# Attention plus a channel MLP on one core: the last 64 keys of a head scored into both partition halves, and q and k loaded whole

## The chip, the cores and the metric

One core of a Trainium2 chip runs the whole program. The metric is the device time of one execution in microseconds (us); the number before is the median of three runs. Engines are named as in the profile: PE is the matrix engine (PEld its weight loads), DVE the vector engine, ACT the scalar engine, POOL GpSimd, SP the engine that issues the DMAs. A "product" is one matmul instruction or, where two matmuls on two halves of the array run side by side, that pair.

## The reference, cut to what matters

```python
def _attn_ref(q, k, v):                    # q, k, v: (8, 12, 448, 64) float32
    scores = 1/np.sqrt(64) * np.matmul(q, k.transpose(0, 1, 3, 2)) - np.log(448)
    attn = 1.0 / (1.0 + np.exp(-scores))   # a sigmoid, no sum over the keys
    return np.matmul(attn, v)
def _moe_ref(x, U, V, w_ch1, w_ch2):       # x: (8, 448, 768), the 12 heads side by side
    h = x.transpose(0, 2, 1) @ U @ V       # rank 32 over the sequence
    u = x + h.transpose(0, 2, 1)
    return u + np.maximum(u @ w_ch1, 0.0) @ w_ch2     # 768 -> 3072 -> 768
```

Eight batches; in each 12 heads, taken as 6 pairs; 448 keys and 448 queries of 64 numbers.

## The kernel before

**Precision.** PE multiplies 16-bit numbers in one pass. A 32-bit factor is therefore split into a high and a low 16-bit part, and a product is made of three: high by high, high by low, low by high. Batches 0 to 2 skip the split in their attention and multiply 32-bit numbers directly ("whole"); batches 3 to 7, 30 pairs, use the split.

**Attention of one pair of heads** (`pair`). The two heads lie in the two halves of the 128 partitions, 64 numbers of a head in each. `loads` fetches k and q by five transfers: k and q of each head (64 rows each) and v. For a split pair ACT measures sums of magnitudes (`bound`), two small transfers through DRAM bring a scale to all partitions (`scale_by_dma`), POOL makes the high parts and DVE the low parts, into a staging tile `stg`. The 448 keys are cut into three blocks of 128 (j = 0, 1, 2) and a block of 64 (j = 3). `scores_of` makes the scores of a block, keys on the partitions, queries along the row, for both heads: for j < 3 into two banks of the accumulator memory (a buffer of `TWO`, one bank per head), for j = 3 into one bank, with head 0 in the partitions 0 to 63 and head 1 in 64 to 127. It is called for the blocks (3, 0) and then for (1, 2). ACT turns the scores into sigmoids (L642), ACT makes their high part (L662) and DVE the low part (L663, recorded under the helper's line 408). `values_of` (L552) then multiplies with v: three products of 128 x 128 for j = 3 (v holds the two heads' 64 keys as a block diagonal), and three products for each j < 3, each of two 128 x 64 matmuls, one per head: 12 products.

**Rank-32 mixing** (`mix`, `mix_half`) follows when six (or three) pairs are done. In `mix_half` a transposing DMA (L798) takes part.

**The MLP.** Batches 0 to 3 go through groups of 18 and 12 matmuls of 128 x 128 by 448 (`ffn_in`, `ffn_out`); the weights arrive as 64-bit words, are decoded (`decode`) and kept in DRAM in split form. Batches 4 to 7 go through a fast multiplication scheme of 7 instead of 8 block products at the end (`in_quad`, `out_quad`), whose inputs are formed early for batches 4 and 5 (`far_forms`, `near_forms`) and whose weight sums are made on POOL (`quarter_sums`). The MLP matmuls of one batch are what PE runs between the attention steps of later batches.

**What sets the order.** `Plan` collects every operation with its engine, a guessed cost, what it reads and writes and a priority `pos`; `Plan.order` walks through time with these costs and writes one fixed order of instructions for each engine. Every engine then runs its own list strictly in order and waits where data is missing. The constants at the top (START, DECODE, PREP, AHEAD and so on) place the priorities. The costs steer the order only; they are no part of the program that runs. Buffers (`QK`, `V32`, `STG`, `A2`, `A1`, `AT2`, `AT1`, the banks `BANK` and `TWO`) are given out by the same walk. Of the banks, 0 to 2 serve the MLP and 3 to 7 attention and mixing from batch 2 on; `TWO[2:]` are banks 4-5 and 6-7.

Transfers are all issued by SP, in its order. The line of a transfer in the profile is often that of the helper `load` (L379), that of a matmul always L395, that of a DVE remainder or POOL scaling L408 or L405: tile names tell them apart.

Of the kernel before, what the change touches and what calls it, by code (L numbers as in the profile page):

```python
# [52 lines left out]
WHOLE = 3  # L53
D2, TWO_AT = 28.077, 81.576
PLAIN = 4
LATER = [4, 3, 5, 6, 7]
TOGETHER = (2, 3, 4, 5)
BEND = 0.096
DIRECT = ()
FORMS = {1: (0,), 2: (1,), 3: (2,)}  # L60
MM = 0.190
TINY = 235

ROOM0, ROOM, AHEAD, BEFORE, D1, SOONER = 65.569, 34.316, 67.823, 41.157, 3.106, 71.183
PREP, BOUNDS, VALUES, SECOND, MIXED = 23.415, 9.75, 1.292, 4.05, 6.82
LOW_POOL = ()
MIXED1, MIX_1 = 9.523, 3.666
MIX_2, EV_IN, EV_OUT, A_OFF = 7.323, 25.524, 4.098, -0.681
START, DECODE = 53.869, 35.813
U_AT, U_STEP = 3.333, 5.172  # L70
LEAD, SUMS, STEP_K, STEP_I, FFN_LEAD = 8.152, 14.538, 16.739, 13.37, 4.0
# [22 lines left out]
class Plan:  # L94
# [13 lines left out]
    def op(self, eng, cost, fn, reads=(), writes=(), pos=0.0, slack=0.0, land=0.12, after=(), port=False):  # L108
# [19 lines left out]
        self.ops.append((eng, cost, fn, sorted(deps), pos, slack, land, tiles, port))  # L128
        return i

    def order(self):
# [10 lines left out]
        ready, end = [0.0] * n, [0.0] * n  # L142
# [6 lines left out]
        done, port, landed = [], 0.0, [0.0] * 8  # L149
# [21 lines left out]
        while len(done) < n:  # L171
            best = None
            for e, c in cand.items():
                now = []
                for i in c:
                    r = room(i)
                    if r is not None:
                        o = self.ops[i]
                        now.append((max(free[e], ready[i], r[0] + o[5] if r[1] else 0.0, port if o[8] else 0.0, landed[-8] if e == "SP" else 0.0), o[4], i))
# [17 lines left out]
            end[i] = t + o[1]  # L197
            free[e] = end[i]
            if o[8]:
                port = end[i]  # L200
            if e == "SP":
                landed.append(end[i] + o[6])
            done.append(i)
            for x in o[7]:
                x.left -= 1
                x.got.free = max(x.got.free, end[i] + o[6])
                if not x.left:
                    x.got.live = False
            for u in users[i]:
                x = self.ops[u]  # L210
                at = end[i] + (o[6] + x[5] if x[0] != e or e == "SP" else 0.0 if e == "PE" else 0.06)
# [34 lines left out]
def fused_kernel(ctx: ExitStack, tc: tile.TileContext, q, k, v, wu, wv, w1, w2, out):  # L246
# [40 lines left out]
    a_, at_ = buf("a", [12 * S], F32), buf("at", [5 * S], F32)  # L287
    A2, A1 = [Buffer(a_[:, 2 * i * S : 2 * (i + 1) * S]) for i in range(5)], [Buffer(a_[:, i * S : (i + 1) * S]) for i in (10, 11)]
    AT2, AT1 = [Buffer(at_[:, 2 * i * S : 2 * (i + 1) * S]) for i in range(2)], [Buffer(at_[:, 4 * S :])]
    QK = ring("qk", 3, [2, S], F32)  # L290
# [30 lines left out]
    for x, owners in ((STG[0].ap, STG[:1]), (STG[1].ap, STG[1:]), (at_.bitcast(F16), AT2 + AT1), (US[1].ap.rearrange("p a b c -> p (a b c)"), US[1:])):  # L321
# [30 lines left out]
    for x in QK + A2 + A1 + V32 + STG + AT2 + AT1:  # L352
# [25 lines left out]
    def load(dst, src, n, reads, writes, pos, land=2.0):  # L378
        op("SP", max(0.6, n / 0.30e6), lambda: nc.sync.dma_start(out=dst(), in_=src()), reads, writes, pos, land=land)  # L379
# [20 lines left out]
    def pe(cost, fn, reads, writes, pos, slack=0.8, after=()):  # L400
        return op("PE", cost, fn, reads, writes, pos, slack, 0.3, after)
# [31 lines left out]
    def scale_by_dma(parts, kp, n, name, pos):  # L433
# [3 lines left out]
        load(lambda: far.x, lambda: parts.x[:, :n], 0.18e6, kp, [far], pos, 4.5)  # L437
        load(lambda: row.x[:, : n * P], lambda: far.x.rearrange("p n -> (p n)").partition_broadcast(P), 0.2e6, [far], [row], pos, 5.0)
        m, x = (lambda: e.x[:, :n]), (lambda: e.x[:, n : 2 * n])
        dve(0.15 + n * 0.13, lambda: nc.vector.tensor_reduce(  # L440
# [67 lines left out]
    def shifted(at):  # L508
        pool(0.5, lambda: nc.gpsimd.memset(ux, 0.0), (), ["ux", "vraw"], at)
        dve(0.25, lambda: nc.vector.tensor_copy(ux[0:64, 0], ua[0:64, 3]), [("ua", i) for i in range(4)] + ["ux"], ["ux"], at)  # L510
        load(lambda: ux[64:128, :, 3], lambda: ua[0:64, :, 0], 0.18e6, [("ua", 0), "ux"], ["ux"], at, 4.5)
        load(lambda: ux[0:64, 1:4, 3], lambda: ua[64:128, 0:3, 0], 0.18e6, [("ua", 0), "ux"], ["ux"], at, 4.5)
# [10 lines left out]
    def loads(b, p, early):  # L523
        qk, v32 = plan.tile("qk", QK), plan.tile("v", V32)
        for h in range(2):
            for i, src in ((1, k), (0, q)):
                load(lambda i=i, h=h: qk.x[rows_of(h), i, :], lambda src=src, h=h: src[b, p, rows_of(h), h, :],
                     D * S * 4, [], [(qk, i, h)], early)
        load(lambda: v32.x, lambda: v[b, p], P * 512 * 4, [], [v32], early + 0.1)
        return qk, v32, [(qk, i, h) for i in range(2) for h in range(2)]  # L530

    def scores_of(b, js, products, kp, pos, early):

        sc = {}
        for j in js:
            if j < 3:
# [3 lines left out]
        n = 1 if b < WHOLE else 3  # L540
# [8 lines left out]
        scored.append(pe(len(js) * (4 if b < WHOLE else 3) * MM + 0.2, fn, kp, list(sc.values()), pos, after=values_ops[-2:-1] + scored[-1:]))  # L549
        return sc  # L550

    def values_of(b, products, tiles, kp, pos):  # L552
        av = plan.tile("av", PS_[b], False)

        def fn():
            n = len(products())
            for i, (x, y) in enumerate(products()):
                matmul(av.x[:, :S], x[:, 3, :], y(tiles[3], 0), start=i == 0, stop=False, skip_group_check=True)
            for j in range(3):
                for i, (x, y) in enumerate(products()):  # L560
# [787 lines left out]
```

## Time and profile before

| what | value |
|---|---|
| time, three runs | 1582.74, 1580.14, 1585.16 us; median 1582.74 |
| the profiled execution: its time / its span | 1585.82 / 1584.0 us |
| mean granted PE clock | 0.997 |
| PE busy | 1566.2 us, 99% of the span |
| DVE, ACT, POOL busy | 1093.3, 755.3, 341.2 us |
| DMA engines' busy share | 61.7% |

The page gives busy time per engine; another view gives the same for stretches of the span; the timeline gives start times of instructions, merged where neighbours are alike. Matmuls overlap in their records (each is shown with some 350 ns), so that the pace of PE is read from start to next start and not from the duration.

The stages of the span are roughly: until 105 us the start (attention of batches 0 and 1, first weights decoded), 105 to 360 us the MLP with batches 1 and 2 in between, 360 to 1000 us the MLP of batches 0 to 3 with the split attention of batches 3 to 7 in between, then to the end the MLP of batches 4 to 7.

### The profile page before, as it was taken

To read this page: it belongs to the slowest core of one execution; us is meant where nothing else is said; L and a number is where in the kernel's file an instruction comes from. 1 tells how busy PE (TensorE), PEld (TensorE's weight loads), DVE (VectorE), ACT (ScalarE), POOL (GpSimd) and SP (SyncE) were. 2 spreads that over 40 slices of the span, in tenths; PEclk is the share of its full clock that TensorE was granted. 3 is DMA by queue.
4 is the path that set the end of the run, shared out by engine and by line. 5 is a ranking of instruction groups with operands and counts; after the bars stand their busy time and mean duration, and the time that the engine had idled before them with its cause. 6 is when DMAs were issued, how large, how long until landed. Compare 5 with 4: busy or idle time off the path is not lost.

```text
span 1584.0 us, 23059 instructions
## 1 busy us (share of the span) xinstructions
PE 1566.2 (99%) x8621; PEld 760.2 (48%) x8621; DVE 1093.3 (69%) x1831; ACT 755.3 (48%) x1269; POOL 341.2 (22%) x429
## 2 busy tenths in 40 slices
PE   8999999999999999999999999899999999999999
PEld 3334544444444444444444444455555555555554
DVE  3787986747667666766568688577677677565656
ACT  6475454534574656655747667242323514121210
POOL 0100000003454351121433211045662500000000
PEclk9999999999999999999999999999999999999999
DMA  8598786525768686855566685877684563323321
GB/s 241 164 313 282 208 265 214 215 63 168 213 189 219 198 248 174 196 190 167 175 196 198 194 213 174 249 257 235 201 259 145 212 235 124 128 105 131 113 105 70
DMA packets 204112, 302.80 MB, mean 191 GB/s; under 512 B 124896, under 2 KB 171104, under 8 KB 192736
## 3 DMA queue, kind: packets, MB, share of 16 engines
q1 hardware_dynamic: 204000, 301.34, 61.7%
q8 instruction: 67, 1.10, 0.3%
q14 instruction: 45, 0.37, 0.1%
HBM read 231.11 MB, written 76.04 MB: 194 GB/s over the span
## 4 chain that ended last, share of the span: by engine, by line
PE 91%; DMA 4%; DVE 3%; ACT 1%; SPq 1%; issue 1%; POOL 0%; DVEq 0%; ACTq 0%
PE banks L395 90%; DMA w<-w_in 1%; DMA v__104<-v_in 1%; PE banks L398 1%; DVE stg__109 L408 0%; DMA w<-parked 0%; DVE a L408 0%; DMA qk__102<-ufar 0%; DMA at<-ufar 0%; DVE tiny L465 0%; ACT at L642 0%; DVE at L408 0%; DMA qk__103<-q_in 0%; DMA a<-ufar 0%; SPq L798 0%
## 5 line engine op out<-in xcount | busy, mean ns | idle before, releaser
L395 PEld LDWEIGHTS <-w__91 128*128 128x128 f16 x1683 | 163.4, 98 | 163.0 <-issue 12.1
L395 PEld LDWEIGHTS <-w__93 128*128 128x128 f16 x1620 | 156.3, 98 | 154.0 <-issue 12.1
L395 PEld LDWEIGHTS <-w__92 128*128 128x128 f16 x1620 | 157.1, 98 | 151.8 <-issue 7.3
L395 PEld LDWEIGHTS <-w__94 128*128 128x128 f16 x1557 | 150.1, 98 | 149.5 <-issue 14.0
L395 PE MATMUL banks<-h__96,w__94 128*128 128x448 f16 x753 | 152.5, 353 | 1.2 <-ACT h__95 L896 1.2
L395 PE MATMUL banks<-h__95,w__93 128*128 128x448 f16 x762 | 153.7, 353 | 0.0
L408 DVE SCALAR_TENSOR_TENSOR a<-at,a 128x448 f16<-128x448 f32 (+1 forms) x120 | 120.0, 1024 | 21.9 <-ACT a L662 21.8
L642 ACT ACTIVATE at<-banks,tiny 128x448 f32<-128x448 f32 (+1 forms) x120 | 115.6, 1002 | 33.7 <-PE banks L395 23.0
L971 POOL TENSOR_TENSOR w<-w 128x384 f32<-128x384 f32 x96 | 105.3, 1097 | 5.5
L395 PE MATMUL banks<-us__89,w__91 128*128 128x448 f16 x492 | 99.5, 353 | 0.0
L395 PE MATMUL banks<-us__90,w__91 128*128 128x448 f16 x492 | 99.4, 353 | 0.0
L395 PE MATMUL banks<-us__89,w__92 128*128 128x448 f16 x489 | 99.2, 353 | 0.0
L395 PE MATMUL banks<-us__90,w__92 128*128 128x448 f16 x489 | 99.0, 353 | 0.0
L662 ACT ACTIVATE a<-at 128x448 f16<-128x448 f32 (+1 forms) x120 | 97.6, 854 | 0.3
L405 POOL TENSOR_SCALAR tiny<-tiny 128x1 f32<-128x1 f32 (+1 forms) x90 | 25.7, 295 | 315.6 <-DVE tiny L405 286.8
L642 ACT ACTIVATE a<-banks,tiny 128x448 f32<-128x448 f32 (+1 forms) x72 | 62.8, 910 | 21.1 <-PE banks L395 18.2
L967 POOL TENSOR_TENSOR w<-w 128x384 f32<-128x384 f16 x48 | 46.5, 995 | 100.7 <-DVE xnt L975 63.2
L895 ACT ACTIVATE r__97<-banks 128x448 f32<-128x448 f32 x48 | 25.9, 540 | 71.2 <-PE banks L395 69.6
L895 ACT ACTIVATE r__98<-banks 128x448 f32<-128x448 f32 x48 | 25.9, 540 | 69.5 <-PE banks L395 69.3
L395 PEld LDWEIGHTS <-stg__108 64*128 64x128 f16 (+3 forms) x675 | 32.6, 102 | 43.1 <-issue 23.1
L395 PEld LDWEIGHTS <-stg__109 64*128 64x128 f16 (+3 forms) x675 | 32.3, 102 | 43.4 <-issue 23.9
L974 ACT CAST xnt<-w 128x1536 f16<-128x1536 f32 x24 | 35.2, 1467 | 32.5 <-POOL w L971 31.9
(927 smaller groups left out, 2811.8 us busy)
## 6 DMA issues: line engine op xcount, KB each, us to landing
w<-w_in SPq DMA_DIRECT2D x48, 768.0 KB, 5.2
forms<-xnt SPq DMA_DIRECT2D x24, 768.0 KB, 4.6
w__91<-forms SPq DMA_DIRECT2D x13, 1344.0 KB, 5.7
w__92<-forms SPq DMA_DIRECT2D x12, 1344.0 KB, 5.7
w__93<-forms SPq DMA_DIRECT2D x12, 1344.0 KB, 5.8
w__94<-forms SPq DMA_DIRECT2D x11, 1344.0 KB, 5.7
forms<-scratch SPq DMA_DIRECT2D x144, 96.0 KB, 3.7
w__91<-scratch SPq DMA_DIRECT2D x7, 1536.0 KB, 7.2
```

What stands on the lines that cost most here:

```text
L395: plan.made.append(nc.tensor.matmul(*x, **y))
L398: plan.made.append(nc.tensor.transpose(**x))
L405: return eng.tensor_scalar(out=out, in0=in_, scalar1=s1, scalar2=s2, op0=op0, **kw)
L408: return nc.vector.scalar_tensor_tensor(out=out, in0=in0, scalar=s, in1=in1, op0=op0, op1=op1)
L642: act(cost, lambda: nc.scalar.activation(out_(), in_(), AF.Sigmoid, bias=bias_s, scale=c if whole else c.x), kin + ["bias"] + kc, kout, pos)
L662: act(0.57 if j == 3 else 0.95, lambda a=a, to=to: nc.scalar.activation(half(a, 0), to.x, AF.Copy, scale=A_UP), kto, [(a, 0)], here + A_OFF)
L895: act(0.54, lambda: nc.scalar.activation(r.x, ph.x[:, :S], AF.Relu, scale=DOWN_H), [ph], [r], pos - EV_IN)
L967: pool(1.0, lambda j=j: nc.gpsimd.tensor_tensor(out=t.x[:, j], in0=quarter(j, 0), in1=quarter(j, 1), op=ALU.add), [(w, j, 0), (w, j, 1)] i ...
L971: pool(1.0, lambda o_=o_, x=x, y=y, sub=sub: nc.gpsimd.tensor_tensor(out=t.x[:, o_], in0=t.x[:, x], in1=t.x[:, y], op=ALU.subtract if sub ...
L974: act(1.45, lambda: nc.scalar.copy(o.x[:, :, :, 0], t.x.rearrange(order)), [(t, j) for j in range(4)], [(o, 0)], pos)
```

## The change

1. For the 30 split pairs ("stacked" in the code) the block j = 3 is treated as a block of 128 keys: the last 64 keys stand twice, in the rows 0 to 63 and 64 to 127. The scores of j = 3 therefore go to a two-bank buffer, one bank per head, with the same scores in both partition halves. The sigmoid and the high part are made over 896 columns of 128 partitions instead of 448. The low part then replaces the high part in the partitions 64 to 127 only, so that one 16-bit tile holds the high part above the low part. v's block for j = 3 holds the same 64 keys in both halves, both heads side by side. A product with it sums high and low part at once, so that v's high part and v's low part suffice: 2 products of two 128 x 64 matmuls each. `values_of` has 2 + 9 = 11 products.
2. k gets 64 more columns in its tile for the copy of the last keys; POOL and DVE scale 512 columns of k instead of 448.
3. q and k come in one transfer each of 128 rows instead of two of 64 rows. For stacked pairs three small transfers are added: the last 64 keys again (128 rows of 256 bytes), and v's last keys into each half (64 rows of two times 256 bytes). v's main transfer has three blocks instead of four.
4. The buffer `AT1` is gone; j = 3 takes its sigmoid tile from `AT2`.
5. `Plan` changes: a cost SWITCH for a change of the matmul's array shape on PE and a priority bonus TURN for it; transfers are planned as one pipe with a rate (RATE) and a landing time (LAND) behind cheaper issues on SP; many costs and nearly all constants have new values, and batch 3 is attended before batch 4. So the order of the instructions on all engines changes.

The whole pairs (batches 0 to 2), the MLP and the mixing have the same instructions as before, in another order.

```diff
-WHOLE = 3
+WHOLE = (6, 6, 6, 0, 0, 0, 0, 0)
-LATER = [4, 3, 5, 6, 7]
+LATER = [3, 4, 5, 6, 7]
+SWITCH, TURN, LAND, RATE = 0.09, -0.873, 2.2, 0.33e6
...
-    def loads(b, p, early):
+    def loads(b, p, early, stacked):
         qk, v32 = plan.tile("qk", QK), plan.tile("v", V32)
-        for h in range(2):
-            for i, src in ((1, k), (0, q)):
-                load(lambda i=i, h=h: qk.x[rows_of(h), i, :], lambda src=src, h=h: src[b, p, rows_of(h), h, :],
-                     D * S * 4, [], [(qk, i, h)], early)
-        load(lambda: v32.x, lambda: v[b, p], P * 512 * 4, [], [v32], early + 0.1)
+        def heads(src, first, n):
+            x = src[b, p]
+            return bass.AP(x.tensor, x.offset + first, [[D * 2 * S + S, 2], [2 * S, D], [1, n]])
+
+        for i, src in ((1, k), (0, q)):
+            load(lambda i=i: qk.x[:, i * S : i * S + S], lambda src=src: heads(src, 0, S), P * S * 4, [], [(qk, i)], early)
+        if stacked:
+            load(lambda: qk.x[:, 2 * S :], lambda k=k: heads(k, S - D, D), P * D * 4, [], [(qk, 2)], early)
+        if stacked:
+            x = v[b, p]
+            ends = bass.AP(x.tensor, x.offset + 384, [[512, D], [512 * D + D, 2], [1, D]])
+            load(lambda: v32.x[:, :3], lambda: v[b, p, :, :3], P * 384 * 4, [], [(v32, 0)], early + 0.1)
+            for i in range(2):
+                load(lambda i=i: v32.x[rows_of(i), 3, :], lambda: ends, D * P * 4, [], [(v32, 1 + i)], early + 0.1)
+        else:
+            load(lambda: v32.x, lambda: v[b, p], P * 512 * 4, [], [(v32, 0), (v32, 1), (v32, 2)], early + 0.1)
...
-                        o = sc[j].x[:, h, :S] if j < 3 else sc[j].x[rows_of(h), :S]
-                        matmul(o, x[rows_of(h), j * P : min(S, j * P + P)], y[rows_of(h)], start=i == 0, stop=i == n - 1)
+                        keys = x[rows_of(h), j * P : j * P + P if stacked else min(S, j * P + P)]
+                        o = sc[j].x[:, h, :S] if j < 3 or stacked else sc[j].x[rows_of(h), :S]
+                        matmul(o, keys, y[rows_of(h)], start=i == 0, stop=i == n - 1)
...
-                matmul(av.x[:, :S], x[:, 3, :], y(tiles[3], 0), start=i == 0, stop=False, skip_group_check=True)
+                if stacked:
+                    for h in range(2):
+                        matmul(av.x[rows_of(h), :S], x[:, 3, rows_of(h)], y(tiles[3], h), start=i == 0, stop=False, skip_group_check=True)
...
+                if j == 3:
+                    return [(part(n), lambda t, h: t.x.bitcast(F16)[:, h * S : (h + 1) * S]) for n in (4, 5)]
...
-            act(0.57 if j == 3 else 0.95, lambda a=a, to=to: nc.scalar.activation(half(a, 0), to.x, AF.Copy, scale=A_UP), kto, [(a, 0)], here + A_OFF)
-            dve2(0.63 if j == 3 else 1.16, lambda a=a, to=to: rest(half(a, 1), to.x, A_UP, half(a, 0)), kto + [(a, 0)], [(a, 1)], here + A_OFF)
+            if j == 3:
+                act(0.95, lambda a=a, to=to: nc.scalar.activation(a.x.bitcast(F16), to.x, AF.Copy, scale=A_UP), kto, [(a, 0)], here + A_OFF)
+                dve2(1.16, lambda a=a, to=to: rest(a.x.bitcast(F16)[D:], to.x[D:], A_UP, a.x.bitcast(F16)[D:]), kto + [(a, 0)], [(a, 1)], here + A_OFF)
...
-        op("SP", 1.0, lambda: nc.sync.dma_start_transpose(out=xt.x, in_=xs.x.rearrange("p c x s -> p (c x s)")),
-           [(xs, i, x) for i in range(3) for x in range(2)], [xt], pos + 1.0, land=7.0)
+        op("SP", 3.7, lambda: nc.sync.dma_start_transpose(out=xt.x, in_=xs.x.rearrange("p c x s -> p (c x s)")),
+           [(xs, i, x) for i in range(3) for x in range(2)], [xt], pos + 1.0, land=LAND, dma=0.9)
```

More of the change, by code (lines that the diff above doesn't have):

```diff
@@ L106, in tile, with op @@
         return t
-    def op(self, eng, cost, fn, reads=(), writes=(), pos=0.0, slack=0.0, land=0.12, after=(), port=False):
+    def op(self, eng, cost, fn, reads=(), writes=(), pos=0.0, slack=0.0, land=0.12, after=(), port=False, dma=0.0, shape=(0, 0)):
         deps = set(after)
@@ L141, in order @@
                 t.left = len(t.users)
-        ready, end = [0.0] * n, [0.0] * n
+        ready, end, down = [0.0] * n, [0.0] * n, [0.0] * n
         free, cand = {}, {}
@@ L178, in order @@
                         o = self.ops[i]
-                        now.append((max(free[e], ready[i], r[0] + o[5] if r[1] else 0.0, port if o[8] else 0.0, landed[-8] if e == "SP" else 0.0), o[4], i))
+                        t = max(free[e], ready[i], r[0] + o[5] if r[1] else 0.0, port if o[8] else 0.0, landed[-8] if e == "SP" else 0.0)
+                        now.append((t, o[4] + (TURN if e == "PE" and o[10][0] != shape else 0.0), i))
                 if now:
@@ L197, in order @@
             end[i] = t + o[1]
+            if e == "PE":
+                end[i] += SWITCH if o[10][0] != shape else 0.0
+                shape = o[10][1]
             free[e] = end[i]
+            down[i] = end[i] + o[6]
             if o[8]:
@@ L201, in order @@
             if e == "SP":
-                landed.append(end[i] + o[6])
+                pipe = max(pipe, end[i]) + o[9]
+                down[i] = pipe + o[6]
+                landed.append(down[i])
             done.append(i)
@@ L205, in order @@
                 x.left -= 1
-                x.got.free = max(x.got.free, end[i] + o[6])
+                x.got.free = max(x.got.free, down[i])
                 if not x.left:
@@ L645, in pair @@
         sc = {}
+        early = b == 0 or b == 1 and p < 2
         for n, j in enumerate((3, 0, 1, 2)):
@@ L725, in mix @@
                     pe(0.66, lambda tp=tp, w=w, sc=sc, x32=x32: matmul(
-                        tp.x[:RANK, :384], uraw[:w, sc], x32(), start=sc == 0, stop=sc == 3), [xn, "uraw"], [tp], at)
+                        tp.x[:RANK, :384], uraw[:w, sc], x32(), start=sc == 0, stop=sc == 3), [xn, "uraw"], [tp], at, shape=(4, 4))
                     continue
@@ L950, in quarter_sums @@
                 op("SP", 0.6, lambda n_=n_, r=r, c=c, x=x: nc.sync.dma_start(out=far(n_, x), in_=cut(far_w, r, c, x)),
-                   [("scratch", i, g)], [("forms", i, n, n_, x)], pos, land=3.0, after=copy_after)
+                   [("scratch", i, g)], [("forms", i, n, n_, x)], pos, land=LAND, after=copy_after, dma=0.49)
                 done.append(("forms", i, n, n_, x))
@@ L957, in quarter_sums @@
                 for x in range(2):
-                    op("SP", 0.7, lambda j=j, r=r, c=c, x=x: nc.sync.dma_start(out=w.x[:, x, j], in_=cut(far_w, r, c, x)),
-                       [("scratch", i, g)], [(w, j, x)], pos - 8, land=2.5, after=after)
+                    op("SP", 0.5, lambda j=j, r=r, c=c, x=x: nc.sync.dma_start(out=w.x[:, x, j], in_=cut(far_w, r, c, x)),
+                       [("scratch", i, g)], [(w, j, x)], pos - 8, land=LAND, after=after, dma=0.42)
         else:
@@ L1012, in get @@
             t, b, part = place(), (b0, b1)[n], c + 3 * r
-            op("SP", 0.8, lambda: nc.sync.dma_start(out=t.x, in_=parked[b][:, part]), [("parked", b, part)], [t], at[0], land=2.5)
+            op("SP", 0.43, lambda: nc.sync.dma_start(out=t.x, in_=parked[b][:, part]), [("parked", b, part)], [t], at[0], land=LAND, dma=0.7)
             act(0.66, lambda: nc.scalar.activation(t.x, t.x, AF.Copy, scale=su.x), [t, su], [t], at[0])
@@ L1049, in near_forms @@
                 f = fs[n, c] = spot("uf", NEXT if first else EARLY)
-                op("SP", 0.6, lambda f=f, n=n, c=c: nc.sync.dma_start(out=f.x, in_=ufar[:, n - 1, c]), [("ufar", n, c)], [(f, 0), (f, 1)], pos, land=2.3, after=scored[-1:] if first else after)
+                op("SP", 0.44, lambda f=f, n=n, c=c: nc.sync.dma_start(out=f.x, in_=ufar[:, n - 1, c]), [("ufar", n, c)], [(f, 0), (f, 1)], pos, land=LAND, after=scored[-1:] if first else after, dma=0.7)
         return fs
@@ L1058, in u_forms @@
                 b, part, t = (b0, b1)[n], c + 3 * r, spot("u")
-                op("SP", 0.8, lambda t=t, b=b, part=part: nc.sync.dma_start(out=t.x, in_=parked[b][:, part]),
-                   [("parked", b, part)], [t], at - 3, land=2.5, after=after)
+                op("SP", 0.4, lambda t=t, b=b, part=part: nc.sync.dma_start(out=t.x, in_=parked[b][:, part]),
+                   [("parked", b, part)], [t], at - 3, land=LAND, after=after, dma=0.7)
                 act(0.6, lambda t=t: nc.scalar.activation(t.x, t.x, AF.Copy, scale=su.x), [t, su], [t], at)
```

151 lines of the change are left out of this document (81 added, 70 removed).

## The prediction, as put on record before the run

> **What bounds the kernel now.** I read the page first, then the stretches, what PE waited for, and the timeline of PE.
>
> ```profile
> span 1584.0 us, 23059 instructions
> PE 1566.2 (99%) x8621; PEld 760.2 (48%) x8621; DVE 1093.3 (69%) x1831; ACT 755.3 (48%) x1269; POOL 341.2 (22%) x429
> PE 91%; DMA 4%; DVE 3%; ACT 1%; SPq 1%; issue 1%; POOL 0%; DVEq 0%; ACTq 0%
> ```
>
> PE is busy nearly throughout and holds 91% of the chain that ended last. Where it is not:
>
> ```profile
> core 0: us, PE busy (x) PEld busy (x) DVE busy (x) ACT busy (x) POOL busy (x), PEclk, DMA share, GB/s
> 0.00:105.00 105.00, 97.39 (x397) 35.02 (x398) 66.11 (x119) 60.23 (x95) 11.69 (x18) 0.97 0.72 232
> 105.00:360.00 255.00, 254.66 (x1298) 120.20 (x1297) 187.44 (x333) 132.93 (x235) 5.65 (x7) 1.00 0.65 211
> 360.00:1000.00 640.00, 638.08 (x3896) 307.79 (x3895) 448.46 (x758) 393.80 (x654) 204.93 (x290) 1.00 0.70 195
> 1000.00:1033.00 33.00, 28.68 (x142) 14.20 (x140) 22.00 (x39) 8.82 (x17) 0.37 (x1) 0.95 0.88 266
> 1033.00:1584.00 551.00, 547.35 (x2894) 282.98 (x2892) 369.33 (x583) 159.51 (x270) 118.55 (x114) 1.00 0.49 165
> ```
> ```profile
> PE banks L395 <- DMA qk__101<-q_in: 4.2, 1, 4.2
> PE banks L398 <- DVE ua__72 L752: 2.4, 1, 2.4
> PE banks L395 <- DMA at<-ufar: 2.0, 3, 1.0
> PE banks L395 <- DMA v__104<-ufar: 2.0, 1, 2.0
> PE banks L395 <- ACT h__95 L896: 1.2, 1, 1.2
> ```
>
> In 360 to 1000 us, where all 30 split pairs lie, PE idles 1.9 of 640 us; ACT works 62% of it, DVE 70%. So in that stage a matmul slot that goes is a slot off the end, unless something new makes PE wait. The five waits listed (us in total, times, longest) sum to 11.8 us. They lie at the start and around 1000 us; they can shrink or grow with the order.
>
> The pace of PE, from the start of one merged row to the start of the next:
>
> ```profile
> 389.19 1.43 PE L395 MATMUL banks<-stg__109 64*64 64x448 f16 x12
> 390.55 3.58 PE L395 MATMUL banks<-us__89,w__92 128*128 128x448 f16 x18
> 394.06 1.31 PE L395 MATMUL banks<-stg__109 64*128 64x448 f16 x12
> 395.30 4.71 PE L395 MATMUL banks<-h__96,w__93 128*128 128x448 f16 x24
> ...
> 412.10 2.55 PE L395 MATMUL banks<-a,stg__109 128*128 128x448 f16 x21
> 414.59 2.44 PE L395 MATMUL banks<-h__95,w__94 128*128 128x448 f16 x12
> 416.87 0.27 PE L398 MATMUL banks<-ident,tiny 128*128 128x128 f32 x1
> ```
>
> Twelve MLP matmuls take 416.87 - 414.59 = 2.28 us: one slot is 0.190. The scores of blocks (1, 2) are 6 pairs, so 6 slots: 1.14 of the 1.24 us seen; the extra is the change of array shape. The scores of (3, 0), 6 slots with 64*64 before 64*128, take 1.36. The values (3 + 9 slots, 2.28) take 2.49.
>
> **The change part by part.**
>
> *Scores.* With j = 3 as 64*128, the call for (3, 0) has the form that the call for (1, 2) has now: 1.24 instead of 1.36, 0.12 us less. *Values.* 11 slots instead of 12: 0.190 less. They still enter from 128*128 and leave to it, with the inner shape change moved to the front, so I count no gain for it; had it a price of its own, the bound is the 2.49 - 2.28 = 0.21 us of all shape changes in the call, either way. Number of pairs:
>
> ```profile
> L395 PE MATMUL banks<-stg__109 64*64 64x448 f16 x90 | 11.3, 357 | 0.0
> L395 PE MATMUL banks<-a,stg__109 128*128 128x448 f16 x45 | 11.0, 354 | 0.0
> ```
>
> 90 = 15 pairs times 6 on this staging buffer, 45 = 15 times 3; the other buffer has as many. So PE loses 30 x (0.12 + 0.19) = **9.3 us**.
>
> *Evacuation of j = 3.* Durations by width (ACT sigmoid, ACT high part, DVE low part):
>
> ```profile
> L642 ACT ACTIVATE at<-banks,tiny 128x896 f32<-128x896 f32 x90 | 96.1, 1096 | 21.1 <-PE banks L395 10.9 <-DVE a L408 7.1 <-DVE ua__73 L408 2.4
> L642 ACT ACTIVATE at<-banks,tiny 128x448 f32<-128x448 f32 x30 | 21.6, 721 | 12.6 <-PE banks L395 12.1
> L662 ACT ACTIVATE a<-at 128x896 f16<-128x896 f32 x90 | 83.1, 949 | 0.2
> L662 ACT ACTIVATE a<-at 128x448 f16<-128x448 f32 x30 | 17.1, 570 | 0.1
> L408 DVE SCALAR_TENSOR_TENSOR a<-at,a 128x896 f16<-128x896 f32 x90 | 101.2, 1143 | 12.1 <-ACT a L662 11.9
> L408 DVE SCALAR_TENSOR_TENSOR a<-at,a 128x448 f16<-128x448 f32 x30 | 20.0, 667 | 9.8 <-ACT a L662 9.8
> ```
>
> ACT gains 0.375 + 0.379 = 0.754 us a pair, 22.6 in all: 393.8 becomes 416 of 640, 65%. DVE gains 0.476 a pair, 14.3 in all: 448.5 becomes 463, 72%. (64 partitions instead of 128 might be cheaper; I assume not.) Neither is near full; I take 0 on the path because PE has MLP chains to run meanwhile; if that cover were gone, the whole 1.23 us a pair would stand on it, 36.9 us.
>
> *Two banks more.* The (3, 0) scores now need both two-bank buffers. The pair's earlier scores must have been read by two sigmoids (2 x 1.10). Between the calls at 389.19 and 394.06 lie 4.87 us, of which 1.36 are scores: 3.5 for 2.2 of sigmoids. I take 0; upper end 1.1 a pair, 33 us.
>
> *Scaling k over 512 columns.* The nearest rows are POOL's, for 448 and 512 columns:
>
> ```profile
> L405 POOL TENSOR_SCALAR stg__109<-qk__103,tiny 128x448 f16<-128x448 f32 x10 | 7.7, 782 | 1.6 <-DVE tiny L444 1.5
> L405 POOL TENSOR_SCALAR stg__108<-v__105,tiny 128x512 f16<-128x512 f32 x15 | 11.1, 740 | 56.6 <-PE banks L395 50.4 <-ACT a L662 6.2
> ```
>
> No more for 512 columns; two DVE remainders at 448 to 896 columns (0.667, 1.143) give about 0.07 us a pair. POOL is 32% busy: nothing.
>
> *Transfers.* A pair has five issues now, a stacked one six (k, q, k's end, v, two v ends), a whole one three.
>
> ```profile
> L379 SPq DMA_DIRECT2D qk__101<-q_in x32: 466/588/1662, 1.4 to 884.8; - x32
> L379 SPq DMA_DIRECT2D qk__101<-k_in x32: 465/530/1415, 0.7 to 884.1; - x32
> L379 SPq DMA_DIRECT2D v__104<-v_in x24: 328/358/626, 3.3 to 925.3; - x24
> ...
> qk__101<-q_in SPq DMA_DIRECT2D x32, 112.0 KB, 3.0
> v__104<-v_in SPq DMA_DIRECT2D x24, 256.0 KB, 3.3
> forms<-scratch SPq DMA_DIRECT2D x144, 96.0 KB, 3.7
> ```
>
> SP spends 2 x 0.588 + 2 x 0.530 + 0.358 = 2.59 us on a pair's issues; six issues are 2.1 at v's price and 3.5 at q's, so -0.5 to +0.9 a pair (a whole pair: -1.5 to -0.8). I take v's for the four of 128 rows and q's for the two of 64: 2.6, no change. What is queued behind them on SP are weight fetches and parked sums that nobody waits for in this stage (0 PE idle put down to them). Landing: 224 KB whole should land in about 3.3 us as v's 256 KB do; the small ones, by the 96 KB copies in small pieces, in up to 3.7. All feed work that begins long after: the loads are placed over 30 us ahead. Cost 0. The first load is exposed (4.2 us): two transfers instead of four, -0.5 to +0.5.
>
> *The new order.* It can take away at most the 11.8 - 4.2 = 7.6 us of the other waits plus what the clock lost beside them (0.97 of 105 us, 0.95 of 33 us, together 4.8); the planner now gives the transposing DMA 3.7 us of SP instead of 1.0, and around 1000 us such DMAs do stand between loads. It can also add; nothing in this trace bounds that above, the nearest are the same 7.6 us doubled. I take 0.
>
> Sum: -9.3. The profiled execution took 1585.82, 3.1 above the median, so 1576.5 in its own terms and **1573.4** against the median 1582.74; I say 1573.
>
> **The rivals.**
>
> *A, forecast:* 9.3 us go, waits change by some us either way: 1568 to 1578.
>
> *B, the order also heals:* 7.6 to 12.4 us at most beside the 9.3, so from 1561; say 1562 to 1568. For it: the waits are few and named. Against: each needs its own remedy.
>
> *C, given back:* the order adds 5 to 14 us, as much as there is now at the start and around 1000 us: 1578 to 1587.5, no change. For it: all constants move at once. Against: PE holds 638 of 640 us in the stage in question.
>
> *D, slower by the longer chain of j = 3:* scores, sigmoid, high part, low part and values follow one another, and ACT and DVE run in order, so MLP evacuations queue behind the wider ones. Each pair must lose 0.31 us to eat the gain, 0.47 for slower by 0.3% (4.75 us, about what a measurement of this kernel tells from no change). With half of the 1.23 us exposed: +18.5, 1592; with all, 1610. Against it: 35% of ACT and 28% of DVE stay free.
>
> *E, slower by whole loads that few DMA engines carry:* the source of a whole q or k load is walked as 2 heads of 64 rows, its outermost count is 2, where now it is 64 (q, k) or 128 (v). If the transfer is dealt out by that count, two of the 16 engines carry all of it.
>
> ```profile
> q1 hardware_dynamic: 204000, 301.34, 61.7%
> ```
>
> 61.7% of 16 x 1584 us for 301.34 MB is 51.9 us of one engine per MB, so 11.9 us for 229 KB, 6 on each of two. Per pair q and k put 11.9 us on those two engines, now 1.5 on each: 10.4 more, every 640/30 = 21.3 us, 0.49 on top of a share of 0.70. At 1.19 they fall behind by 0.19 x 640 = 122 us: 1695. Packets may run quicker when the other engines are idle, and queues forgive something, so 1600 to 1700. It decides once the two engines are full, from a further 0.30 of share. For it: the code. Against: no transfer in this trace has so small an outer count, so nothing shows that dealing goes by it; if all 16 carry it, A stands. The Trainium skill, "DMA: Bandwidth & Descriptors", section "Why a DMA increments its semaphore by 16 and not by 1", says that the hardware picks at most 16 engines by what divides the slowest dimension that is not 1 on both sides; by that rule the number is 2 and E is the forecast, 1695 at the worst instead of 1573. No run here shows it yet.
>
> **How the numbers follow.** A 0.56, B 0.10, C 0.08, D 0.06, E 0.20. The likeliest is A, 1573, its own range 1568 to 1578. From 1562 to 1598 the range holds A to D, 0.80, and leaves E out. Faster is A and B: 0.66; same is C and a bit of D: 0.09; slower is the rest of D and E: 0.25.
>
> **What would show it.** Right: no 64*64 or 128*128 matmuls on `stg` in 16 bits, scores of (3, 0) 1.24 us from start to next start, values 2.30, 30 more matmuls in the values but PE busy about 1557; all 120 sigmoids of split pairs at 896 columns near 1.10 us; PE idle under 3 us between 360 and 1000. D: PE waits on ACT L642 or DVE `a` there, some tenths of a us thirty times. E: q and k landing 7 us or more after issue instead of 3, ACT's `junk` and PE waiting for q_in and k_in. C: new waits on DMA at the start or near 1000 us. What would make me wrong is above all E, and an order that starts the MLP late.

## The result, and the profile after

| | median (lowest to highest), us | ratio to before, 95% |
|---|---|---|
| before, beside these runs | 1583.95 | 1 |
| after | 1856.48 (1855.59 to 1858.85) | 1.1727 [1.1701, 1.1752] |
| forecast | 1573 (1562 to 1598) | |

The change made the kernel 273 us slower. The head of the page of after, with the chain by engine and by line and the main DMA queue:

```profile
span 1853.8 us, 23175 instructions
PE 1618.3 (87%) x8651; PEld 780.1 (42%) x8651; DVE 1103.6 (60%) x1831; ACT 774.7 (42%) x1269; POOL 341.3 (18%) x429
q1 hardware_dynamic: 213660, 302.31, 52.6%
PE 56%; DMA 25%; DVE 7%; SPq 6%; ACT 3%; issue 2%; POOL 0%; ACTq 0%; DVEq 0%
```

PE falls from 99% to 87% of the span, and from 91% to 56% of the chain; DMA takes 25% of the chain and SP's own issuing 6%. The same queue moves nearly the same bytes (302.31 MB instead of 301.34), and its 16 engines are less busy on average (52.6% instead of 61.7%). So the chip is not short of bandwidth in total; something is late.

The transfers of q in after (issue time min/median/max in ns; then first and last start in us), and who waited for them (us, times):

```profile
L387 SPq DMA_DIRECT2D qk__101<-q_in x16: 529/554/8763, 1.5 to 1096.6; - x16
L387 SPq DMA_DIRECT2D qk__102<-q_in x16: 515/568/7857, 5.6 to 1122.4; - x16
L387 SPq DMA_DIRECT2D qk__103<-q_in x16: 514/558/8722, 15.9 to 1149.6; - x16
  ACT junk L469: 85.0, 17
  PE banks L403: 28.9, 4
```

An issue that takes 0.55 to 0.57 us at the median takes up to 8.8. ACT's `junk` operation, which sums squares of q, k and v for their scales, waits 85.0 us for q, 132.2 for k and 64.6 for v in all; in the kernel before these were 0.4, 8.0 and 23.2. The sign that the prediction named for E, a landing 7 us or more after the issue, can't be read off the profile of after, which has no landing times. The first load gives one: q was issued at 1.5 us, and PE, which waited for it, began at 13.2. The timeline of SP in after shows the pattern: k passes, the q behind it stands for eight microseconds, and what SP has next stands behind it.

```profile
28.47 0.53 SPq L387 DMA_DIRECT2D qk__101<-k_in  x1
29.05 8.17 SPq L387 DMA_DIRECT2D qk__101<-q_in  x1
37.33 4.75 SPq L387 DMA_DIRECT2D w<-w_in  x1
42.13 0.46 SPq L387 DMA_DIRECT2D v__104<-v_in  x1
42.69 0.53 SPq L387 DMA_DIRECT2D qk__102<-k_in  x1
43.26 4.52 SPq L387 DMA_DIRECT2D qk__102<-q_in  x1
```

Counted over the whole trace and leaving out the transposing DMAs, 111 issues of after last longer than 1.5 us, 416 us in all; of before 15, 29 us. Only 11 of the 111 are q; 24 are k or its end, 22 are v and 13 the weights `w_in`, so SP also stands at transfers that are not two-headed. What PE waits for is then mostly not the DMA itself: of its 235.5 us of idle time 37 are put down to a DMA, 66 to DVE and 124 to ACT, which stood in its own order behind `junk`. From the waits of after (us in total, times, longest):

```profile
PE banks L403 <- ACT at L675: 66.1, 21, 10.2
PE banks L406 <- DVE tiny L864: 29.9, 4, 20.9
PE banks L403 <- ACT h__96 L935: 20.9, 2, 13.3
PE banks L403 <- DMA qk__101<-q_in: 18.6, 2, 13.2
ACT junk L469 <- DMA qk__101<-k_in: 57.0, 8, 9.9
DVE tiny L448 <- DMA row__114<-far: 62.8, 17, 12.9
```

The last two rows stand for one class each: inputs that land late, and other transfers (a scale's round trip through DRAM) that are late too, although their own patterns were not changed.

### The profile page after: what moved, and what is told of

The parts are those of the page before. It is cut to its first block, busy times and chain, and to the rows that moved or that the text cites. A ratio compares the mean times of both kernels' runs of the same rounds, so it can differ in the third digit from the quotient of the medians.

```text
span 1853.8 us, 23175 instructions
## 1 busy us (share of the span) xinstructions
PE 1618.3 (87%) x8651; PEld 780.1 (42%) x8651; DVE 1103.6 (60%) x1831; ACT 774.7 (42%) x1269; POOL 341.3 (18%) x429
## 3 DMA queue, kind: packets, MB, share of 16 engines
q1 hardware_dynamic: 213660, 302.31, 52.6%
## 4 chain that ended last, share of the span: by engine, by line
PE 56%; DMA 25%; DVE 7%; SPq 6%; ACT 3%; issue 2%; POOL 0%; ACTq 0%; DVEq 0%
PE banks L403 55%; DMA w<-w_in 7%; SPq L387 5%; DMA row__114<-far 3%; DMA qk__101<-q_in 3%; DMA qk__102<-q_in 3%; DMA v__104<-v_in 2%; DMA v__105<-v_in 2%; DMA far<-tiny 2%; DVE a L416 1%; ACT at L675 1%; DMA scratch<-w__93 1%; DMA w<-u_in 1%; DMA w<-w 1%; DMA qk__103<-q_in 1%
## 5 line engine op out<-in xcount | busy, mean ns | idle before, releaser
L403 PEld LDWEIGHTS <-w__91 128*128 128x128 f16 x1620 | 161.2, 100 | 182.3 <-issue 45.2
L403 PEld LDWEIGHTS <-w__92 128*128 128x128 f16 x1683 | 165.7, 99 | 162.4 <-issue 15.9
L403 PEld LDWEIGHTS <-w__93 128*128 128x128 f16 x1557 | 153.6, 100 | 179.5 <-issue 49.8
L403 PEld LDWEIGHTS <-w__94 128*128 128x128 f16 x1620 | 158.3, 99 | 162.6 <-issue 22.1
L416 DVE SCALAR_TENSOR_TENSOR a<-at,a 64x896 f16<-64x896 f32 (+1 forms) x120 | 134.5, 1133 | 58.2 <-ACT a L698 47.6
L403 PE MATMUL banks<-h__95,w__93 128*128 128x448 f16 x675 | 144.9, 368 | 19.7 <-DVE ua__71 L416 11.5
L403 PE MATMUL banks<-h__96,w__94 128*128 128x448 f16 x705 | 147.3, 360 | 7.6 <-ACT h__95 L935 4.8
L675 ACT ACTIVATE at<-banks,tiny 128x896 f32<-128x896 f32 x120 | 127.2, 1093 | 30.7 <-DVE a L416 19.3
L413 POOL TENSOR_SCALAR tiny<-tiny 128x1 f32<-128x1 f32 (+1 forms) x90 | 30.0, 343 | 588.1 <-DVE tiny L413 520.5
L403 PE MATMUL banks<-us__89,w__91 128*128 128x448 f16 x498 | 112.2, 380 | 17.6 <-ACT h__96 L935 13.3
L403 PE MATMUL banks<-us__90,w__91 128*128 128x448 f16 x498 | 104.5, 360 | 0.0
L403 PE MATMUL banks<-us__89,w__92 128*128 128x448 f16 x495 | 104.4, 363 | 0.0
L403 PE MATMUL banks<-us__90,w__92 128*128 128x448 f16 x492 | 102.4, 358 | 0.0
L701 ACT ACTIVATE a<-at 128x896 f16<-128x896 f32 x90 | 83.8, 949 | 0.8 <-PE banks L403 0.4
L403 PE MATMUL banks<-stg__109 64*128 64x448 f16 x360 | 46.6, 390 | 36.6 <-ACT at L675 29.0
L403 PE MATMUL banks<-stg__108 64*128 64x448 f16 x360 | 46.3, 390 | 33.7 <-ACT at L675 28.2
L403 PEld LDWEIGHTS <-stg__109 64*128 64x128 f16 (+1 forms) x690 | 35.4, 104 | 79.5 <-issue 59.9
L403 PEld LDWEIGHTS <-stg__108 64*128 64x128 f16 (+1 forms) x690 | 36.0, 105 | 78.0 <-issue 58.7
L448 DVE TENSOR_REDUCE tiny<-row__114 128x3 f32<-128x384 f32 x30 | 20.1, 669 | 62.9 <-DMA row__114<-far 62.8
```

The lines of the kernel that those rows point to most:

```text
L403: plan.made.append(nc.tensor.matmul(*x, **y))
L413: return eng.tensor_scalar(out=out, in0=in_, scalar1=s1, scalar2=s2, op0=op0, **kw)
L416: return nc.vector.scalar_tensor_tensor(out=out, in0=in0, scalar=s, in1=in1, op0=op0, op1=op1)
L448: dve(0.15 + n * 0.175, lambda: nc.vector.tensor_reduce(out=m(), in_=row.x[:, : n * P].rearrange("q (p n) -> q n p", n=n), axis=AX.X, op=A ...
L675: act(cost, lambda: nc.scalar.activation(out_(), in_(), AF.Sigmoid, bias=bias_s, scale=c if whole else c.x), kin + ["bias"] + kc, kout, pos)
L701: act(0.95, lambda a=a, to=to: nc.scalar.activation(half(a, 0), to.x, AF.Copy, scale=A_UP), kto, [(a, 0)], here + A_OFF)
```

## The experiments

The first question is whether the whole loads cost the 273 us, and by what. The second, smaller one is where the 9.3 us that stacking should free have gone. Theory E of the prediction: a transfer is dealt to the DMA engines by the outermost count of its access pattern, here 2.

### The loads: `rows64`, `rows128`, `before_whole2`

`rows64` keeps all of the changed kernel and its order, but issues each q, k and k's end as two transfers of 64 rows. `rows128` keeps one transfer each, but q and k are laid in DRAM so that a pair is 128 rows in a row. `before_whole2` is the kernel before with nothing but the whole loads of q and k from two heads (it has no k's end).

```diff
-            return bass.AP(x.tensor, x.offset + first, [[D * 2 * S + S, 2], [2 * S, D], [1, n]])
+            return bass.AP(x.tensor, x.offset + first, [[S, P], [1, n]])      # rows128
...                                                                            # and the host's layout of q and k
```

> The changed kernel with each whole transfer of q, k and k's end issued as two of 64 rows (outermost count 64 instead of 2); order of every engine as changed. Theory 'two engines' (a source whose outermost count is 2 is carried by two DMA engines, and SP stands still behind it): the loss is gone, 1573 us (1566 to 1582), PE idle in the middle of the span below 5 us. Rival 'order' (the new order makes PE wait, the transfers are innocent): still above 1840. Rival 'stacking' (longer evacuation of j = 3, three small transfers): still above 1840.

> The changed kernel with q and k laid out by the host as 128 contiguous rows per pair, so that one whole transfer has the outermost count 128; instructions and order as changed. 'Two engines': 1572 us (1563 to 1580), SP's issue of q and k near 0.35 us. 'Whole transfers are bad as such' (one long transfer on one queue): above 1800. 'Order' and 'stacking': above 1840.

> The kernel before with one edit: q and k of a pair come in one transfer each of 2 heads of 64 rows (outermost count 2), in the place of the first half; everything else and the order as before. 'Two engines': the loss of the changed kernel and the 9.3 us of PE work that are not saved, about 1584 + 272 + 9 = 1865 us (1800 to 1900). 'Order' or 'stacking': 1584.

Measured: rows64 1596.19 us, 1.0082 [1.0060, 1.0103]; rows128 **1576.80**, 0.9960 [0.9940, 0.9980]; before_whole2 1813.07, 1.1450 [1.1419, 1.1481]. With rows128 the order of the instructions on every engine is that of after; only the source's pattern differs, and 280 us go. Two-headed loads of q and k put into the kernel before cost 230. So the loads are the cause, whatever the rest of the change does. Rows64 takes away 260 us, but stays 14 us above the range that was expected of it, and PE idles 23.9 us in its middle stretch where below 5 had been expected; no run shows why.

The transfers of q in rows128:

```profile
L387 SPq DMA_DIRECT2D qk__101<-q_in x16: 332/420/871, 1.2 to 841.3; - x16
  ACT junk L469: 9.1, 6
  PE banks L403: 4.1, 1
DMA to landing us min/median/max: 2.5/4.8/8.9
```

How many engines carry such a load can be counted in the trace's DMA packets. A row of q or k is a packet of 1792 B; so many of them were in flight at once during the first 150 us:

```
kernel    outermost count   most of the time that any were in flight      highest
after     2                 2 (98 of 118 us)                              4
outer4    4                 4 or 5 (67 of 82 us)                          7
outer16   16                spread over 1 to 20                           21
rows128   128               spread over 1 to 19                           19
before    64 (two halves)   spread over 1 to 20                           21
```

(outer4 and outer16 follow below.) This is what the Trainium skill, "DMA: Bandwidth & Descriptors", section "Why a DMA increments its semaphore by 16 and not by 1", states: the number of engines is the largest up to 16 that divides the slowest dimension that is not 1 on both sides. The trace agrees, with 2 and 4 packets in flight most of the time for counts of 2 and 4.

Where the time is lost can be read from stretches that hold the same work in each kernel: up to the first score of a split pair, from there to the last values, and the rest. The rows give PE's busy time and count first; the last three columns are PE's clock, the DMA share and GB/s. After:

```profile
core 0: us, PE busy (x) PEld busy (x) DVE busy (x) ACT busy (x) POOL busy (x), PEclk, DMA share, GB/s
0.00:475.50 475.50, 388.63 (x1789) 169.17 (x1791) 273.84 (x506) 200.47 (x343) 27.27 (x41) 0.91 0.55 177
475.50:1253.50 778.00, 633.54 (x3715) 302.72 (x3714) 433.03 (x689) 402.46 (x635) 196.69 (x274) 0.91 0.52 149
1253.50:1853.80 600.30, 596.14 (x3154) 308.21 (x3150) 396.72 (x637) 171.79 (x291) 117.35 (x115) 1.00 0.51 173
```

rows128:

```profile
0.00:369.30 369.30, 364.78 (x1789) 163.36 (x1791) 275.33 (x506) 203.86 (x351) 27.96 (x41) 1.00 0.70 232
369.30:980.30 611.00, 594.51 (x3715) 291.02 (x3714) 430.55 (x689) 401.35 (x628) 196.61 (x274) 0.99 0.65 187
980.30:1580.60 600.30, 596.14 (x3154) 308.21 (x3150) 397.27 (x637) 171.87 (x291) 117.56 (x115) 1.00 0.51 173
```

PE's counts are the same row by row (1789, 3715, 3154). After loses 106.2 us in the first stretch, 167.0 in the second, and nothing in the third, where no q or k is loaded. Of the 273.2 us, 62.9 are PE's own busy time (1618.3 against 1555.4): the same matmuls at a granted clock of 0.91 instead of 1.00. The other 210.3 are idle time.

### The dose: `outer4`, `outer16`, `q_two_k_halves`, `whole18_two`

`outer4` and `outer16` are after with q and k laid in 4 groups of 32 rows, or 16 of 8, and a row of gap behind each group. `q_two_k_halves` is after with k by halves of 64 rows and q still from two heads. `whole18_two` is rows64 with only the 18 whole pairs loaded from two heads.

```diff
...                                  # the pattern within heads(), and the host's layout
-[[D * 2 * S + S, 2], [2 * S, D], [1, n]]
+[[33 * S, 4], [S, 32], [1, n]]      # outer4
+[[9 * S, 16], [S, 8], [1, n]]       # outer16
```

> The changed kernel, q and k laid out by the host in 4 groups of 32 rows with a gap behind each, so that the source of a whole transfer has the outermost count 4; order as changed. Theory 'the outermost count is the number of engines': four engines carry a load, three to four us instead of six; the extra share on those is 0.25 instead of 0.5, so most of the loss goes but not all: 1630 us (1590 to 1720). If only a count of 16 or more rids of the loss for another reason (strides, gaps): still above 1830. If any layout by rows would do: 1577.

> The changed kernel with k (and its end) issued as two transfers of 64 rows as in rows64, and q still whole from 2 heads of 64 rows: half the bytes on the two engines. Theory 'the two engines are full': their extra share falls from 0.5 to 0.25, 0.95 in all, so the loss falls by far more than half: 1600 to 1670 us. Rival 'each transfer costs its own wait' (SP's standstill and the landing, per transfer): half of the loss stays, 1725 us (1700 to 1760).

> The changed kernel with q and k laid in 16 groups of 8 rows with one row of gap after each group, so that the outermost count of a load is 16; every engine's order as in the changed kernel. Theory (the outermost count decides how many DMA engines carry a load; outer4 gave 1684, an outermost count of 2 gave 1856): all 16 engines share it, 1572 to 1585, as rows128 with 1577. Rival (the gaps in the source, not the count, made outer4 slow): 1640 or more, with issues by SP of over 1.5 us in dozens.

> rows64 (1596) with q and k of the 18 whole pairs alone loaded from two heads of 64 rows, as in the changed kernel; the 30 later pairs keep two transfers of 64 rows each. Every engine's order as in rows64. Theory now (the loss is local: what the changed kernel lost by the first split score, 475.5 against 374.2 us in rows64, 101 us, comes from these 18 pairs): 1690 to 1705, with the first split score near 475 us and the stage after it as long as in rows64. My prediction's own count (only the split stage can lose, since only it was priced): 1596 to 1605. Rival by bytes with the saturation that q_two_k_halves showed (half the bytes kept 37 % of the loss, so 18/48 keep some 25 %): about 1660.

Measured: outer4 1684.44 us, 1.0649 [1.0629, 1.0668]; q_two_k_halves 1692.68, 1.0701 [1.0678, 1.0724]; outer16 1584.01, 1.0001 [0.9987, 1.0016]; whole18_two 1693.55, 1.0683 [1.0667, 1.0699].

Outer16 clears the gaps and leaves the count as the cause; it is still 0.4% slower than rows128 (intervals apart), which no run takes apart. Outer4 lies in its wide range but 54 us above the number expected, q_two_k_halves between the ranges of its two theories, neither of which stands. These two kernels came out close to one another: twice the engines, or half the bytes on two engines, keep 108 of 280 us over rows128 and 97 of 260 us over rows64, 38% and 37%. So the loss goes with the work that each loaded engine gets, neither all or nothing nor in proportion. The stretches of outer4 show it in both stages (38 us and 63 us above rows128):

```profile
0.00:407.70 407.70, 373.70 (x1787) 165.79 (x1787) 274.63 (x506) 200.84 (x344) 27.25 (x41) 0.97 0.67 208
407.70:1081.70 674.00, 614.51 (x3713) 296.23 (x3714) 434.44 (x689) 401.50 (x635) 196.78 (x274) 0.96 0.61 171
```

In whole18_two the loss stays where the two-headed loads are: 466.1 us up to the first split score, where rows64 has 374.2, and 625.7 in the split stage against 619.1. Whole18_two, then rows64:

```profile
0.00:466.10 466.10, 387.43 (x1787) 169.40 (x1787) 274.40 (x506) 203.23 (x348) 26.01 (x40) 0.91 0.57 181
466.10:1091.80 625.70, 596.10 (x3713) 291.30 (x3714) 436.12 (x689) 401.33 (x631) 203.03 (x275) 0.98 0.66 184
```
```profile
0.00:374.20 374.20, 365.65 (x1789) 163.35 (x1791) 275.72 (x506) 203.20 (x349) 27.25 (x41) 1.00 0.72 227
374.20:993.30 619.10, 595.16 (x3715) 291.07 (x3714) 433.87 (x689) 401.40 (x629) 197.89 (x274) 0.99 0.66 186
```

The 18 pairs cost 97 us in all, 5.4 each; the 30 split pairs of after cost 167.0 / 30 = 5.6 each, with k's end among their loads. The rival by bytes (1660) falls.

Two things work together in this loss and were not taken apart: the transfer itself lands late, and SP stands still, which delays others' transfers. The long issues sum to 416 us in after, 200 in whole18_two, 90 in outer4 and 83 in q_two_k_halves, for losses of 280, 97, 108 and 97: the two do not go in step, so SP's standing alone does not set the loss.

### Stacking and the order: `rows128_plain`, `before_rows128`, `stack_old_plan`

With healthy loads the rest of the change can be seen. `rows128_plain` is rows128 with no pair stacked (j = 3 as before, 12 products), under the new planner; `before_rows128` is the kernel before, in its own order, with whole loads of 128 rows; `stack_old_plan` is stacking and 128-row loads under the planner and constants of before.

```diff
-        stacked = not direct
+        stacked = False      # rows128_plain
...
```

> As rows128, but without the stacking: j = 3 is scored into one bank and has three products, no small transfers; costs and constants of the changed planner (so the order shifts a little). 'Two engines' with 9.3 us for the stacking: 9 us above rows128, 1582 us (1574 to 1592). 'Stacking' as the cause of the loss: about 1583 while rows128 stays above 1840. 'Order': above 1840.

> The kernel before with one edit: q and k laid out as 128 contiguous rows per pair by the host and loaded whole (in the place of the first half's transfer); order of all engines as before. It gives what whole transfers are worth when all engines carry them. Theory 'hidden': SP's issues shrink from four of 0.55 us to two of 0.35 a pair, but nothing waits for them: 1581 us (1577 to 1585). Rival 'SP was holding things up': 1570 or less.

> The stacked computation and q, k as 128 contiguous rows, but planned by the planner, costs and constants of the kernel before (its transfer costs and no price for array shapes). Theory 'the new plan costs some 10 us' (rows128_plain has the instructions of before and still takes 7.5 us more than before): 1571 us (1566 to 1577), 9 us below before_rows128, below rows128's 1576.8. Rival 'the stacking itself makes PE wait, the plan is innocent': 1577 to 1585, no better than rows128.

Measured: rows128_plain 1590.26 us, 1.0044 [1.0029, 1.0060]; before_rows128 1579.12, 0.9982 [0.9971, 0.9992]; stack_old_plan 1597.60, 1.0108 [1.0091, 1.0124]. Together with rows128:

| whole loads of 128 rows | planner of before | new planner |
|---|---|---|
| not stacked | 1579.1 | 1590.3 |
| stacked | 1597.6 | 1576.8 |

Stacking is worth 13.5 us under the new planner and costs 18.5 under the old one. No single price belongs to the edit; that each planner's constants fit the work that they were set for is the likely reason, but no run shows it. The theory that the new plan as such costs some 10 us falls, and 1597.6 lies above the rival's range too. Best against best of this table, stacking gains 2.3 us, which is not clear of noise (0.9960 and 0.9982, intervals overlapping).

Why it costs under the old order is in part what rival D names. In the profiled executions PE idles 39.0 us in stack_old_plan and 14.3 in before_rows128. The largest waits of PE in stack_old_plan between 360 and 1000 us, where it idles 18.1:

```profile
PE banks L395 <- ACT at L664: 10.0, 8, 2.9
PE banks L395 <- ACT h__95 L924: 2.7, 2, 2.5
PE banks L395 <- ACT h__96 L924: 1.6, 1, 1.6
```

The sigmoids of split pairs (`at`) and the MLP's evacuations (`h`) are late on ACT, 14.3 us together. Some 4.7 of the 10.0 stand before matmuls of scores, which wait for banks that a sigmoid must read first: this is the prediction's term "Two banks more", taken at 0. In rows128 this wait on `at` is 0.9 us in that stretch; there other waits take the place:

```profile
PE banks L403 <- DVE ua__71 L416: 4.6, 1, 4.6
PE banks L403 <- DMA w<-w: 3.8, 1, 3.8
PE banks L403 <- DVE tiny L434: 2.5, 1, 2.5
PE banks L403 <- ACT r__97 L934: 1.4, 1, 1.4
```

The first of them in the timeline of rows128:

```profile
642.52 0.66 DVE L448 TENSOR_REDUCE tiny<-row__114 128x3 f32<-128x384 f32 x1 [5.54 <-DMA row__114<-far]
643.09 0.68 DVE L416 SCALAR_TENSOR_TENSOR ua__71<-banks,tiny,ua__71 128x448 f32<-128x448 f32 x1
643.82 1.65 PE L403 MATMUL banks<-h__95,w__93 128*128 128x448 f16 x4 [4.62 <-DVE ua__71 L416]
```

DVE stands 5.54 us at a reduction whose transfer has not landed; the evacuation that PE needs is next in DVE's order. The planner counts a landing 2.2 us after that transfer is through its planned pipe, and its median from issue to landing, in the list of issues of rows128, is 4.6:

```profile
row__114<-far SPq DMA_DIRECT2D x30, 192.0 KB, 4.6
```

That gave the last theory: landing guesses that are too early cost the missing 7 us.

### The landing guess: `land_far_old`, `land_all_3_2`

```diff
-        load(lambda: far.x, lambda: parts.x[:, :n], 0.08e6, kp, [far], pos)
+        load(lambda: far.x, lambda: parts.x[:, :n], 0.08e6, kp, [far], pos, 4.5)      # land_far_old; the second one 5.0
-SWITCH, TURN, LAND, RATE = 0.09, -0.873, 2.2, 0.33e6
+SWITCH, TURN, LAND, RATE = 0.09, -0.873, 3.2, 0.33e6                                  # land_all_3_2
```

> rows128 with the planner told that the two transfers of a scale through DRAM (row maxima out, broadcast back) land 4.5 and 5.0 us after they are issued, as the kernel before plans them, where the changed one plans 2.2 (the profile of rows128 shows a median of 4.6 us from issue to landing for the broadcast). Content and loads are those of rows128; only the order differs. Theory (planned landings that are too early put reductions and casts in front of evacuations, and PE waits 16.5 us for them between 360 and 1000 us): the wait on the evacuation of ua at 639 us goes, PE's idle time in that stretch falls under 8 us, 1566 to 1573. Rival (the new plan's constants are fitted to each other as they are, any one changed alone costs): 1580 to 1600.

> rows128 with the planner told that every transfer lands 3.2 us after it is through the pipe, in place of 2.2. Theory (too early landings cost): PE's idle time between 360 and 1000 us falls under 8 us, 1566 to 1573. Rival (fitted constants): 1580 to 1600. If both this and land_far_old come out slower, the 7 us that stacking did not bring are not a matter of the landing guess alone.

Measured: land_far_old **1576.04** us, 0.9944 [0.9931, 0.9957]; land_all_3_2 1593.01, 1.0053 [1.0041, 1.0066]. Land_far_old has the lowest median, not told apart from rows128's (the intervals overlap), and the theory does not stand as stated. The wait on `ua__71` is gone, yet PE still idles 14.2 us between 360 and 1000 (rows128: 16.5; less than 8 was expected). Cut by work instead, from the first split score to the last values, the idle time did fall, from 16.5 us to 8.8; behind the last values it rose from 4.2 to 9.6. The row of 360 to 1000, and the largest waits there:

```profile
360.00:1000.00 640.00, 625.78 (x3893) 306.39 (x3891) 454.05 (x731) 408.83 (x644) 198.06 (x280) 0.99 0.68 196
```
```profile
PE banks L403 <- DMA w__94<-scratch: 3.8, 1, 3.8
PE banks L403 <- ACT at L675: 2.4, 1, 2.4
PE banks L403 <- DVE uc__83 L416: 1.8, 1, 1.8
```

And the same correction made to all transfers costs some 15 us against rows128 (1.0053 against 0.9960). The waits are single places in an order that shifts as a whole when one number changes. Land_far_old lies between the two ranges expected, land_all_3_2 in the rival's. Which property of the order lets them come is open.

## Why the prediction was wrong

**The step that failed** is "Landing: ... Cost 0", with the chance of 0.20 on E beside it. The prediction took the price of v's transfer (outermost count 128) for a transfer with an outermost count of 2, because "no transfer in this trace has so small an outer count, so nothing shows that dealing goes by it". The absence of a row was counted as evidence against E, while the whole change of the loads hung on that pattern. The runs show 2 packets in flight most of the time, and 280 us that go with the pattern alone.

**E's price was also too low**: 122 us, 1695 at the worst. Its sum for one pair, 0.70 x 21.3 + 10.4 = 25.3 us of work for each of the two engines, comes near the 778.0 / 30 = 25.9 us that a pair of after takes, in part by luck. With the 0.65 of rows128's split stage in place of before's 0.70 it gives 0.65 x 20.4 + 10.4 = 23.7, and it leaves out k's end. No record names the engine of a packet, so that the two engines were full is not shown. Mis-sized or missing were four terms:

1. Only the 30 pairs between 360 and 1000 us were counted; the 18 whole pairs before them use the same loads, and cost 97 to 106 us. (The sentence that the whole pairs have "the same instructions as before" holds for their computation, not for their loads of q and k.)
2. "Packets may run quicker" lowered the range to 1600; a packet of 1792 B took 74 ns at the median in before and in after.
3. "It decides once the two engines are full, from a further 0.30 of share": outer4 puts 6 - 1.5 = 4.5 us more on an engine per pair, 0.21 of share, and lost 63 us in the split stage and 108 in all, where this says none. By the same sum an engine then has 17.8 us (with 0.65) to 19.4 us (with 0.70 x 21.3) of work in the 20.4 us that a pair of rows128 takes, 87 to 95% (an estimate). So time was lost although the sum leaves the engines some slack.
4. k's end comes from two heads as well, 64 packets of 256 B on an engine at a median of 18 ns, 1.2 us a pair (an estimate). From the first split score to the last values before_whole2, which has no k's end, loses 129 us (733.7 against 604.8 in before), after 167.0; no run changes k's end alone.

**SP's issues, "2.6, no change"**: the prediction took v's 0.358 us for a load of 128 rows; q's median was 0.55 to 0.57 in after, and 0.42 in rows128. What mattered more is that single issues held SP for up to 8.8 us, and that "nobody waits" failed for what stood behind. The first load, "-0.5 to +0.5": PE's first matmul waited 13.2 us for it (the longest wait on q_in above) instead of 4.2.

**What was right**, read in rows128, where the loads are healthy. From the timeline of PE, the scores of (3, 0) and a values call, each with the instruction behind it:

```profile
511.34 1.31 PE L403 MATMUL banks<-stg__108 64*128 64x448 f16 x12
512.58 0.32 PE L406 MATMUL banks<-ident,tiny 128*128 128x128 f32 x1
...
867.77 2.27 PE L403 MATMUL banks<-a,stg__109 128*64 128x448 f16 x22
869.97 2.25 PE L403 MATMUL banks<-us__90,w__92 128*128 128x448 f16 x11
```

Start to start 1.24 us (forecast 1.24) and 2.20 (forecast 2.30; the inner change of array shape, for which it counted no gain, was worth the other 0.10). PE's busy time is 1555.4 us (forecast 1557), 10.8 less than before. The evacuations cost what the rows of 896 columns said, also on 64 partitions:

```profile
L675 ACT ACTIVATE at<-banks,tiny 128x896 f32<-128x896 f32 x120 | 127.3, 1095 | 39.1 <-DVE a L416 17.4 <-PE banks L403 13.7 <-issue 2.6
L416 DVE SCALAR_TENSOR_TENSOR a<-at,a 64x896 f16<-64x896 f32 x30 | 34.6, 1153 | 8.0 <-ACT a L698 7.3
```

**"PE idle under 3 us between 360 and 1000", and the new order at 0**, were wrong without E too: 16.5 us idle in rows128 where before had 1.9. So of the 9.3 us (10.8 measured on PE) 2 to 6 reach the end: 2.3 by the medians of rows128 and before_rows128 (not clear of noise), 6.0 by the ratios of land_far_old and before_rows128 (0.9944 against 0.9982, intervals apart). PE's idle time over the whole span rose from 17.8 us in before to 25.2 in rows128. The upper bound that the prediction took for the order, the 7.6 us of waits doubled, held; its value 0 did not, and the 7.4 us more of idle time lie within the 5 to 14 of rival C.

## What to carry to other kernels

Before joining two transfers into one, look at the slowest dimension of the joined pattern: a count of 2 put the load on two DMA engines (two packets in flight most of the time) and cost 17%, a count of 4 cost 6.5%, and with 16 or 128 nothing was lost against the kernel before. The mean share of the DMA engines does not show it (it fell); long issues on the queue's engine do, and so does ACT's wait for its loads. A cost that no row of the trace shows is not thereby small: price it for every place where the new pattern is used, and let its chance follow from what is known of the mechanism.

## What the runs showed of the hardware that was not expected

- An issue on SP's queue that takes 0.55 us at the median stands for up to 8.8 us in after, and what SP has next stands behind it: 111 issues over 1.5 us, 416 us in all. In rows128, which differs in the source's pattern alone, there are 11, 24 us.
- Loads on few engines cost time before the sum says that these are full (outer4: 108 us at an estimated 87 to 95%).
- The indirect part is large: 62.9 of the 273 us are the same matmuls at a granted clock of 0.91 in the stretches where PE had gaps.
- A whole load of 128 rows issues in a median of 0.42 us, while a load with an outermost count of 4 or 16 takes 0.57 to 0.58, as one of 64 rows does (0.59). Rows64, with two of these per load in place of one of 0.42, is 1.2% slower than rows128 in the same order (1.0082 against 0.9960, intervals apart).
